# Inducing-point attention and routed experts in one pass: logits with tokens on partitions, PSUM as two pairs and four singles, eight chunks of x loaded a second time

## The chip, the cores and the metric

The kernel runs on one core of a Trainium2 chip. The metric is device time in microseconds of one execution; the median of several runs counts. Besides it there is one profiled execution with its trace.

## The reference

`x` is 4 batches of 10048 tokens with 128 channels in float32. 32 inducing vectors attend to all tokens of a batch (`h`), every token then attends to the 32 rows of `h`, and the result goes through a mixture of 16 experts in 4 groups, one expert a token:

```python
h = mab(I, x)            # softmax(scale * I @ x.T) @ x
y = mab(x, h)            # softmax(scale * x @ h.T) @ h
g_idx = argmax(y @ w_group); g_w = softmax(y @ w_group)[g_idx]
e_idx = argmax(y @ w_expert[g_idx]); e_w = softmax(y @ w_expert[g_idx])[e_idx]
out = g_w * e_w * (relu(y @ w1[g_idx, e_idx]) @ w2[g_idx, e_idx])
```

## The kernel before, in words

All arithmetic is float32. A batch is cut into J = 4 strands of 2512 tokens, and these into NK = 5 chunks of KW = 512 tokens; a chunk (b, k) holds 512 tokens of each strand, 1 MB. `xT` holds x with channels on partitions (this is loaded for every chunk, to `xk`, ten buffers), `xm` the same x with tokens on partitions.

Stage one (`att1`, `chunk`) of a chunk: scores of the inducing vectors (line 355), their running maximum (357, 362), the exponential on ScalarE with the sum of the weights in an accumulator (365), four transposes of the weights (373), and the weighted sums of x (391), which need x with tokens on partitions (`xn`, three buffers). Two chunks get `xn` from `xm` by DMA (`LOADED`); for the others `turn` transposes x on TensorE, 16 transposes in two halves (322), each half in two PSUM banks side by side, evicted by ScalarE or VectorE (294), whichever `sooner` names. After five chunks, `common` and `mean` make `hT`, and `routes` the small matrix `rbd` with the router's columns, 9 a strand (32 with padding). All tokens of a batch are expected to choose one expert: `routes` finds it from the mean, `expert` loads its weights, and makes, with the side of the ReLU that each hidden unit is on, a 32 x 128 matrix G (520, 532, 539, 543). Whether all of this holds for each token is checked on the way (counts on GpSimd, 602 to 611, `verdict`); a slow path stands behind for batches where it doesn't.

Stage two (`att2`) of a chunk: scores against `hT` (563), a transpose in blocks of 32 x 32 on VectorE (569), the maximum (573), its subtraction on GpSimd (575), the exponential (577), a second block transpose to `et` (580), the logits by one matmul with `rbd` as weights (585), and a third block transpose (593), after which tokens stand on partitions. `gates` turns logits of one or two chunks into one factor a token (626 to 646), and `outputs` multiplies the weights with it on GpSimd (655), transposes them (661), makes 4 matmuls of 512 columns with G (669) in four PSUM banks, evicts them (294) and writes 1 MB (678).

Nothing of this is in program order. `Plan` steps through generators, one for each job above; a job yields the engine that it wants next. `Pace` holds a modelled time for each engine, with a cost for each instruction; the plan takes the job that can start first, and among those that can start within a small window the one with the lowest key (batch and chunk number, with `LAG` = 9 chunks between a chunk's stage one and its stage two). What comes out is a fixed order for each engine (`in_order`). `Banks` hands out PSUM: four pairs of banks; a job takes a whole pair (`turn`, twice a chunk; `outputs`, two at once) or one bank of any pair, preferably one whose other half is taken:

```python
if n == 2:
    able = [(max(self.done(i, 0), self.done(i, 1)), i, 0) for i in range(4) if not (self.taken[i, 0] or self.taken[i, 1])]
```

Loads and stores all stand in SP's queue. At the start it issues batch 0's five chunks, `xm` of (0, 3) and (0, 4), and three chunks of batch 1; more loads of x are issued only once a first expert's weights have been asked for (`fetched`), then whenever a buffer comes free. SP also waits there for the expert's number (`value_load`, line 512).

Of the kernel before, what the change touches and what calls it, by code (L numbers as in the profile page):

```python
# [41 lines left out]
LOADED = {(0, 3), (0, 4)}  # L42
GROUPS = {b: [(0, 1), (2, 3), (4,)] for b in range(B)}
# [10 lines left out]
class Pace:  # L54
# [15 lines left out]
    def cost(self, i, n):  # L70
# [3 lines left out]
        if kind == "PE":  # L74
            n = math.prod([n for _, n in i.outs[0].ap[1:]])
            if "is_transpose=True" in str(i):
                return 0.11, 0.2
            c = max(0.025, n / 2400 + 0.0025) * (4 if i.ins[0].dtype == F32 else 1)
            rows, cols = i.ins[0].ap[0][1], i.outs[0].ap[0][1]
            return c / (4 if min(rows, cols) == 32 else 1), 0.2  # L80
        if kind == "POOL":
            return 0.1 + n / 500, 0.1
        if kind == "ACT":
            sides = [bool(self.span(x)) for x in i.ins[1:3]]
            return 0.1 + n / 1200 + 0.09 * sum(sides) + 0.2 * (len(outs) > 1), 0.15
        if kind == "DVE":
            return 0.07 + n / 960 + (0.08 if "Recip" in type(i).__name__ and n > 1 else 0.0), 0.13
# [113 lines left out]
class Banks:  # L201


    def __init__(self, pool, pace, pe):
        self.pairs = [pool.tile([P, 2 * KW], F32, name=f"ps{i}") for i in range(4)]
        self.taken = {(i, h): False for i in range(4) for h in range(2)}
        self.pace, self.pe, self.held = pace, pe, {}

    def done(self, i, h):
        return self.pace.idle(self.pairs[i].tensor.name, h * KW, h * KW + KW - 1)  # L210

    def take(self, n=1):
        asked = 0.0
        while True:
            now = max(self.pace.at.get(self.pe, 0.0), asked) + 0.05
            if n == 2:
                able = [(max(self.done(i, 0), self.done(i, 1)), i, 0) for i in range(4) if not (self.taken[i, 0] or self.taken[i, 1])]
            else:
                able = [(self.done(i, h), not self.taken[i, 1 - h], i, h) for (i, h), t in self.taken.items() if not t]
                soon = [x for x in able if x[0] <= now]  # L220
                able = [(t, i, h) for t, _, i, h in (sorted(soon, key=lambda x: (x[1], x[0])) or able)]
            if not able:
                yield
                continue
            t, i, h = able[0] if n == 1 and able[0][0] <= now else min(able)
            if t > now:
                asked = t
                yield t
                continue
            whole = self.pairs[i]  # L230
            tile_ = whole if n == 2 else whole[:, h * KW:(h + 1) * KW]
            for x in range(n):
                self.taken[i, h + x] = True
            self.held[id(tile_)] = tile_, [(i, h + x) for x in range(n)]
            return tile_

    def give(self, t):
        for x in self.held.pop(id(t))[1]:
            self.taken[x] = False


def fast(ctx, tc, xT, xm, wr, w1, w2, out, keep):
# [20 lines left out]
    xnring = Ring(cp, "xn", [P, TK, J, C], 3)  # L263
# [6 lines left out]
    lgring = Ring(cp, "lg", [P, 2, TQ, Q], 2)  # L270
    wring = Ring(cp, "w", [P, 2, TQ], 3)
# [4 lines left out]
    for r in rbd:  # L276
        nc.gpsimd.memset(r, 0.0)
# [5 lines left out]
    cnts = [tl([P, TQ, NL], f"cnt{i}") for i in range(2)]  # L283
    lows = [tl([P, len(GROUPS[b])], f"low{b}") for b in range(B)]

    xks, xns, hTs, hsums, rbds, Gs, es, lgs, ws = {}, {}, {}, {}, {}, {}, {}, {}, {}
    todo_x = list(CHUNKS)

    def sooner():

        return ACT if pace.at.get(ACT, 0.0) <= pace.at.get(DVE, 0.0) else DVE
# [4 lines left out]
    def load_xk(n=1):  # L296
        for _ in range(n):
            if todo_x and xring.tiles:
                b, k = todo_x.pop(0)
                t = xring.tiles.pop(0)  # L300
                nc.sync.dma_start(out=t, in_=xT[b, k])
                xks[b, k] = t

    def load_xn(b, k):
        t = xnring.tiles.pop(0)
        nc.sync.dma_start(out=t, in_=xm[b, k])
        xns[b, k] = t

    def turn(b, k):
# [6 lines left out]
        for half in range(2):  # L316
            ps = yield from banks.take(2)
            ts = range(half * TK // 2, (half + 1) * TK // 2)
            for i, t in enumerate(ts):
                tw = min(P, w - t * P)  # L320
                for j in range(J):
                    nc.tensor.transpose(ps[:tw, (i * J + j) * P:(i * J + j + 1) * P], xks[b, k][:, j, off + t * P:off + t * P + tw], ident)  # L322
            on = sooner()
            yield on
            full = sum((t + 1) * P <= w for t in ts)
            psv = ps.rearrange("p (t j c) -> p t j c", j=J, c=C)
            copy(on, xn[:, ts[0]:ts[0] + full], psv[:, :full])
            if full < len(ts):
                tw = w % P
                copy(on, xn[:tw, ts[-1]], psv[:tw, full])  # L330
            banks.give(ps)
            if half:
# [4 lines left out]
    def att1(b):  # L337
# [4 lines left out]
        if b < 2:  # L342
            small[i] = nbs, tl([P, 1], f"ssum{i}"), tl([P, C], f"hacc{i}"), [tl([P, 1], f"sm{i}{k}") for k in range(NK)], [tl([P, 1], f"cr{i}{k}") for k in range(NK)], tl([P, 1], f"mx{i}")
        nbs, ssum, hacc, sms, crs, mx = small[i]
        fcs = []

        def chunk(k):
# [10 lines left out]
            nb, sm, cr = nbs[k], sms[k], crs[k]  # L358
# [743 lines left out]
```

## Time and profile before

| | us |
|---|---|
| median of 3 runs | 262.26 (261.3 to 269.64) |
| the profiled execution | 261.98 |
| its span, first to last instruction | 260.1 |
| TensorE matmuls busy | 195.9 (75%) |
| VectorE busy | 175.0 (67%) |
| ScalarE busy | 98.7 (38%) |
| GpSimd busy | 60.8 (23%) |
| mean granted clock of TensorE | 0.881 |

Busy times are sums over the whole span; the kernel has stages of different kinds, so the sums are to be read stage by stage. The granted clock is 1.0 at 2.4 GHz and 0.5 at 1.2 GHz.

### The profile page before, as it was taken

The numbers are of one execution on the slowest core, as the hardware profiler recorded it, in microseconds if no ns is written. First come the engines' busy times: TensorE is split into PE (matmuls) and PEld (weight loads), VectorE is DVE, ScalarE is ACT, GpSimd is POOL, SyncE is SP. The second block draws the span as 40 slices with busy tenths as digits, with TensorE's granted clock in tenths as the row PEclk, the third lists the DMA queues.
The fourth block names the chain that finished last, engine by engine and source line by source line (L and its number), as shares of the span: only waits on it lengthen the run. The fifth ranks groups of instructions, "written<-read, shape, count | busy, mean of one in ns | idle before, by whom it ended". The sixth has DMA issues, their size and how long they took to land.

```text
span 260.1 us, 4501 instructions
## 1 busy us (share of the span) xinstructions
PE 195.9 (75%) x1705; PEld 107.3 (41%) x1705; DVE 175.0 (67%) x493; ACT 98.7 (38%) x173; POOL 60.8 (23%) x84
## 2 busy tenths in 40 slices
PE   0687889997989969979998583779979579475430
PEld 0253657653755745334755341234643352111100
DVE  0155647497767757888896959475886999946610
ACT  0444225435346343278620231336835106251420
POOL 0000000032113013432314134213360635344010
PEclk9999999999999988999999898555999959866755
DMA  6999300995003953599057000047343712816434
GB/s 216 427 425 422 160 0 4 319 420 233 3 0 111 372 190 140 178 394 377 8 210 277 0 0 0 1 165 323 161 149 163 267 59 101 355 53 282 202 129 152
DMA packets 12782, 48.42 MB, mean 186 GB/s; under 512 B 1104, under 2 KB 7376, under 8 KB 7888
## 3 DMA queue, kind: packets, MB, share of 16 engines
q1 hardware_dynamic: 12752, 48.05, 47.3%
q8 instruction: 15, 0.25, 0.4%
q14 instruction: 15, 0.12, 0.1%
HBM read 27.47 MB, written 20.58 MB: 185 GB/s over the span
## 4 chain that ended last, share of the span: by engine, by line
PE 48%; DVE 32%; issue 7%; ACT 6%; DMA 3%; SPq 0%; POOL 0%; ACTq 0%; DVEq 0%
PE ps L669 10%; PE ps L322 7%; PE ps L355 7%; PE ps L585 6%; PE ps L391 5%; PE ps L373 4%; PE ps L563 3%; DVE lg L593 3%; DVE mx L357 3%; ACT pe L365 3%; DVE et L580 2%; PE ps L520 2%; PE ps L539 2%; DMA xk<-xT 2%; DVE e L569 2%
## 5 line engine op out<-in xcount | busy, mean ns | idle before, releaser
L575 POOL TENSOR_TENSOR e<-e,mxe 128x512 f32<-128x512 f32 x20 | 20.9, 1047 | 106.8 <-DVE mxe L573 106.7
L669 PE MATMUL ps<-at,G 32*128 32x512 f32 x160 | 35.9, 832 | 9.9 <-DVE at L661 5.5
L294 ACT COPY osb<-ps 128x1024 f32<-128x1024 f32 x32 | 31.1, 1017 | 28.5 <-PE ps L669 18.9
L322 PE MATMUL ps<-cst,xk 128*128 128x128 f32 (+1 forms) x288 | 40.1, 285 | 0.0
L322 PEld LDWEIGHTS ps<-cst,xk 128*128 128x128 f32 (+1 forms) x288 | 33.1, 145 | 13.8 <-issue 8.9
L585 PE MATMUL ps<-et,rbd 128*128 128x512 f32 x40 | 26.4, 752 | 15.5 <-DVE et L580 15.2
L294 ACT COPY xn<-ps 128x1024 f32<-128x1024 f32 (+2 forms) x30 | 27.5, 925 | 25.3 <-PE ps L322 23.1
L655 POOL TENSOR_TENSOR e<-e,w 128x512 f32<-128x512 f32 x20 | 20.6, 1047 | 49.1 <-DVE w L646 49.1
L355 PE MATMUL ps<-xk,indT_sb 128*32 128x512 f32 (+1 forms) x160 | 22.7, 641 | 11.6 <-DMA xk<-xT 7.2
L365 ACT ACTIVATE pe<-ps,nb 128x512 f32<-128x512 f32 (+1 forms) x20 | 13.6, 679 | 34.6 <-DVE nb L362 9.1
L357 DVE TENSOR_REDUCE mx<-ps 128x1 f32<-128x512 f32 (+1 forms) x20 | 13.4, 671 | 17.1 <-PE ps L355 6.2
L391 PE MATMUL ps<-xn,pt 128*32 128x128 f32 (+1 forms) x640 | 21.7, 276 | 1.8 <-DVE xn L294 0.7
L563 PE MATMUL ps<-xk,hT 128*32 128x512 f32 x160 | 19.7, 599 | 2.9 <-ACT pe L365 2.0
L669 PEld LDWEIGHTS ps<-at,G 32*128 32x128 f32 x160 | 11.1, 240 | 25.9 <-issue 8.8
L391 PEld LDWEIGHTS ps<-xn,pt 128*32 128x32 f32 (+1 forms) x640 | 16.4, 109 | 9.3 <-issue 4.8
L569 DVE STREAM_TRANSPOSE e<-ps 128x512 f32<-128x512 f32 x20 | 14.0, 701 | 8.6 <-PE ps L520 3.4
L593 DVE STREAM_TRANSPOSE lg<-ps 128x512 f32<-128x512 f32 x20 | 14.1, 707 | 7.1 <-PE ps L585 1.9
L585 PEld LDWEIGHTS ps<-et,rbd 128*128 128x128 f32 x40 | 7.1, 221 | 25.8 <-DVE et L580 21.3
L661 DVE STREAM_TRANSPOSE at<-e 128x512 f32<-128x512 f32 x20 | 13.9, 698 | 5.1 <-PE ps L669 1.9
L577 ACT ACTIVATE e<-e 128x512 f32<-128x512 f32 x20 | 12.4, 629 | 12.4 <-POOL e L575 12.4
L373 PE MATMUL ps<-cst,pe 128*128 128x128 f32 x80 | 13.2, 295 | 2.7 <-ACT pe L365 1.1
L605 POOL TENSOR_SCALAR hit<-lg 128x128 f32<-128x128 f32 x16 | 8.5, 532 | 23.9 <-DVE lg L593 22.4
(109 smaller groups left out, 241.4 us busy)
## 6 DMA issues: line engine op xcount, KB each, us to landing
xk<-xT SPq DMA_DIRECT2D x20, 1024.0 KB, 8.5
out<-osb SPq DMA_DIRECT2D x16, 1024.0 KB, 3.9
out<-osb SPq DMA_DIRECT2D x4, 928.0 KB, 4.9
xn<-xm SPq DMA_DIRECT2D x2, 1024.0 KB, 15.6
w1s<-w SPq DMA_DIRECT2D x4, 512.0 KB, 3.7
w2s<-w SPq DMA_DIRECT2D x4, 512.0 KB, 6.0
cst<-consts SPq DMA_DIRECT2D x1, 178.5 KB, 2.4
indT_sb<-indT SPq DMA_DIRECT2D x1, 16.0 KB, 1.8
```

Source lines behind the costliest of these rows:

```text
L294: (nc.scalar.copy if engine == ACT else nc.vector.tensor_copy)(out=out, in_=in_)
L322: nc.tensor.transpose(ps[:tw, (i * J + j) * P:(i * J + j + 1) * P], xks[b, k][:, j, off + t * P:off + t * P + tw], ident)
L355: nc.tensor.matmul(ps[32 * j:32 * j + 32, :w], lhsT=indT_sb, rhs=xks[b, k][:, j, off:], start=True, stop=True)
L357: nc.vector.reduce_max(out=mx, in_=ps[:, :w], axis=AX.X)
L365: nc.scalar.activation(out=pe[:, :w], in_=ps[:, :w], func=AF.Exp, bias=nb, scale=SCALE, accum_out=sm)
L373: nc.tensor.transpose(ps[:tw, t * P:(t + 1) * P], pe[:, t * P:t * P + tw], ident)
L391: nc.tensor.matmul(hq[32 * j:32 * j + 32, 0:C], lhsT=pt[:tw, t, 32 * j:32 * j + 32], rhs=xn[:tw, t, j, :], start=(t == 0), stop=(t == nt - 1))
L563: nc.tensor.matmul(ps[32 * j:32 * j + 32, :], lhsT=hTs[b][:, 0:M], rhs=xks[b, k][:, j, :], start=True, stop=True)
L575: nc.gpsimd.tensor_tensor(out=e, in0=e, in1=mx[:, :, None].broadcast_to([P, TQ, M]), op=ALU.subtract)
L585: nc.tensor.matmul(ps, lhsT=rbds[b].rearrange("p j l -> p (j l)"), rhs=et, start=True, stop=True)
L593: nc.vector.transpose(out=slot.rearrange("p t l -> p (t l)"), in_=ps)
L669: nc.tensor.matmul((p0, p1)[j // 2][:, j % 2 * KW:(j % 2 + 1) * KW], lhsT=Gs[b][32 * j:32 * j + 32, :], rhs=at[32 * j:32 * j + 32, :], sta ...
```

## The change

- **Logits.** `et` becomes the weights of four matmuls with `rbd` (36 columns) moving; the result has tokens on partitions at once, 144 columns a chunk, and stays in one PSUM bank for a group of three chunks, then two. The third block transpose goes. The gates are then in another order than the weights that they multiply; four matmuls with an identity of 32 columns bring them back, and a copy takes them out of PSUM.
- **PSUM.** Two pairs and four single banks, each kind for its own takers.
- **x.** Chunks 1 and 3 of every batch come from `xm` too: 8 chunks, in two buffers of their own; `turn` has two buffers. Loads are issued in the order of use whenever a buffer is free, not after the first expert.
- **Sum of weights.** x with tokens on partitions has a 129th column of ones, so the weighted sums carry the sum of the weights; the accumulator and the running sums of VectorE go.
- **Expert.** The product for the second stage is made once, not for each strand; 32 matmuls by column groups take the place of eight.
- **Checks** are made once a group, in a job of their own. **Copies** go to ScalarE unless it is over 1 us behind VectorE. The planner's costs of instructions are other numbers.

```diff
-LOADED = {(0, 3), (0, 4)}
-GROUPS = {b: [(0, 1), (2, 3), (4,)] for b in range(B)}
+LOADED = {(b, k) for b in range(B) for k in (1, 3)}
+GROUPS = [(0, 1, 2), (3, 4)]
+GT = T * max(map(len, GROUPS))
+SPARE = 1.0
+PAIRS = 2
...
-            return c / (4 if min(rows, cols) == 32 else 1), 0.2
+            return max(0.06, c) / (4 if min(rows, cols) == 32 else 1) * 1.1, 0.2
         if kind == "POOL":
-            return 0.1 + n / 500, 0.1
+            return 0.36 + n / 740, 0.15
...
     def __init__(self, pool, pace, pe):
-        self.pairs = [pool.tile([P, 2 * KW], F32, name=f"ps{i}") for i in range(4)]
-        self.taken = {(i, h): False for i in range(4) for h in range(2)}
-        self.pace, self.pe, self.held = pace, pe, {}
+        self.free = {2: [pool.tile([P, 2 * KW], F32, name=f"pp{i}") for i in range(PAIRS)],
+                     1: [pool.tile([P, KW], F32, name=f"ps{i}") for i in range(8 - 2 * PAIRS)]}
...
+            t = min(free, key=self.done)
+            if self.done(t) > now:
+                asked = self.done(t)
+                yield asked
                 continue
+            free.remove(t)
+            return t
...
-    xnring = Ring(cp, "xn", [P, TK, J, C], 3)
+    xnring, xmring = Ring(cp, "xn", [P, TK, J, C + 1], 2), Ring(cp, "xm", [P, TK, J, C + 1], 2)
+    for t in xnring.tiles:
+        nc.gpsimd.memset(t[:, :, :, C:C + 1], 1.0)
...
-    mtring = Ring(cp, "mt", [P, FB, J, M], 1)
-    rbd = [tl([P, J, Q], f"rbd{i}") for i in range(2)]
+    mtring = Ring(cp, "mt", [P, FB, M], 1)
+    rbd = [tl([P, J, NL + 1], f"rbd{i}") for i in range(2)]
...
+    todo = [(what, *c) for c in CHUNKS for what in ("x", "n") if what == "x" or c in LOADED]
...
-        return ACT if pace.at.get(ACT, 0.0) <= pace.at.get(DVE, 0.0) else DVE
+        return ACT if pace.at.get(ACT, 0.0) <= pace.at.get(DVE, 0.0) + SPARE else DVE
...
+    def load():
+        for what, b, k in list(todo):
+            ring, src, have = (xring, xT, xks) if what == "x" else (xmring, xm, xns)
+            if not ring.tiles:
+                continue
+            todo.remove((what, b, k))
+            t = ring.tiles.pop(0)
+            nc.sync.dma_start(out=t, in_=src[b, k])
+            have[b, k] = t
...
-            nc.scalar.activation(out=pe[:, :w], in_=ps[:, :w], func=AF.Exp, bias=nb, scale=SCALE, accum_out=sm)
+            nc.scalar.activation(out=pe[:, :w], in_=ps[:, :w], func=AF.Exp, bias=nb, scale=SCALE)
...
-                    nc.tensor.matmul(hq[32 * j:32 * j + 32, 0:C], lhsT=pt[:tw, t, 32 * j:32 * j + 32], rhs=xn[:tw, t, j, :], start=(t == 0), stop=(t == nt - 1))
+                    nc.tensor.matmul(hq[32 * j:32 * j + 32, 0:C + 1], lhsT=pt[:tw, t, 32 * j:32 * j + 32], rhs=xn[:tw, t, j, :], start=(t == 0), stop=(t == nt - 1))
             ptring.give(pt)
-            xnring.give(xn)
+            (xmring if (b, k) in LOADED else xnring).give(xn)
+            load()
...
-                nc.vector.scalar_tensor_tensor(out=ssum, in0=ssum, scalar=cr, in1=sm, op0=ALU.mult, op1=ALU.add)
-                nc.vector.scalar_tensor_tensor(out=hacc, in0=hacc, scalar=cr, in1=hq[:, 0:C], op0=ALU.mult, op1=ALU.add)
+                nc.vector.scalar_tensor_tensor(out=hacc, in0=hacc, scalar=cr, in1=hq[:, 0:C + 1], op0=ALU.mult, op1=ALU.add)
...
-        fetched.add(b)
-        load_xk(XBUFS)
...
+        nc.vector.tensor_tensor(out=mt, in0=psv, in1=side[:, :, None].broadcast_to([P, FB, M]), op=ALU.mult)
...
-            nc.tensor.matmul(ps[:, 0:C], lhsT=mt[:, n].rearrange("p j m -> p (j m)"), rhs=w2s[:, n, :], start=(n == 0), stop=(n == FB - 1))
+            for j in range(J):
+                nc.tensor.matmul(ps[32 * j:32 * j + 32, 0:C], lhsT=mt[:, n, :], rhs=w2s[:, n, :], start=(n == 0), stop=(n == FB - 1))
...
-        if fetched:
-            load_xk()
+        load()
...
+        if (b, g) not in lgs:
+            lgs[b, g] = yield from banks.take()
+        lg, n = lgs[b, g], GROUPS[g].index(k)
+        for t in range(TK):
+            c = (n * TK + t) * J * (NL + 1)
+            nc.tensor.matmul(lg[:, c:c + J * (NL + 1)], lhsT=et[:, t * P:(t + 1) * P], rhs=rbds[b].rearrange("p j l -> p (j l)"), start=True, stop=True)
...
-        nc.tensor.matmul(ps, lhsT=rbds[b].rearrange("p j l -> p (j l)"), rhs=et, start=True, stop=True)
...
-        nc.vector.transpose(out=slot.rearrange("p t l -> p (t l)"), in_=ps)
...
+        nc.gpsimd.tensor_tensor(out=rq, in0=rs[:, :, None].broadcast_to([P, n * T, J]), in1=own_j[:, None, :, 0].broadcast_to([P, n * T, J]), op=ALU.mult)
...
+        nc.vector.tensor_tensor(out=wq, in0=pr[:, :, None].broadcast_to([P, n * T, J]), in1=rq, op=ALU.mult)
+        yield PE
         ps = yield from banks.take()
+        for j in range(J):
+            nc.tensor.matmul(ps[32 * j:32 * j + 32, 0:n * T], lhsT=same_m[:, 0:Q], rhs=wq.rearrange("p (t j) q -> p t j q", j=J)[:, :, j, :], start=True, stop=True)
+        w = yield from wring.take()
+        yield DVE
+        nc.vector.tensor_copy(out=w[:, 0:n * T], in_=ps[:, 0:n * T])
...
+        plan.add(checks(b, g, x, n), key(b, k) + LAG + 3.0, POOL, pace.at[DVE])
+    def checks(b, g, x, n):
+        cnt, parts = cnts[b % 2], x.rearrange("p (n t) l -> p n t l", n=n)
+        nc.gpsimd.tensor_scalar(x, x, 0.0, None, op0=ALU.is_ge)
...
-        p0 = yield from banks.take(2)
-        p1 = yield from banks.take(2)
+        n = min(PAIRS, 1) + 1
+        pss = []
+        for _ in range(J // n):
+            pss.append((yield from banks.take(n)))
```


## Rows read from the trace of the kernel before

**Rows 1.** The page: its first part's line of engines, and the slices' clock.

```profile
PE 195.9 (75%) x1705; PEld 107.3 (41%) x1705; DVE 175.0 (67%) x493; ACT 98.7 (38%) x173; POOL 60.8 (23%) x84
...
PEclk9999999999999988999999898555999959866755
```

**Rows 2.** Windows by stage: span, busy PE, PEld, DVE, ACT, POOL, clock, DMA, GB/s.

```profile
52.00:143.00 91.00, 81.48 (x822) 47.38 (x818) 71.06 (x207) 39.99 (x72) 23.69 (x30) 0.98 0.55 208
...
143.00:182.00 39.00, 28.06 (x121) 12.45 (x111) 27.58 (x66) 13.16 (x27) 10.79 (x13) 0.69 0.20 82
...
197.00:260.10 63.10, 35.44 (x157) 14.34 (x157) 40.37 (x116) 18.47 (x26) 19.32 (x24) 0.73 0.46 182
...
162.50:181.00 18.50, 15.00 (x47) 6.30 (x49) 10.40 (x20) 8.32 (x14) 4.71 (x5) 0.50 0.39 161
```

**Rows 3.** Timeline of PE (start, duration, line): 90 us, 133 to 178 us, 215 us.

```profile
90.01 2.05 PE L539 MATMUL ps<-w2s,mt 128*128 128x128 f32 x16
...
133.76 1.09 PE L322 MATMUL ps<-cst,xk 128*128 128x128 f32 x8
...
145.41 0.99 PE L355 MATMUL ps<-xk,indT_sb 128*32 128x464 f32 x8 [1.55 <-DVE big L534]
...
150.75 1.02 PE L585 MATMUL ps<-et,rbd 128*128 128x512 f32 x2
...
165.44 3.35 PE L669 MATMUL ps<-at,G 32*128 32x512 f32 x8
...
177.11 1.11 PE L322 MATMUL ps<-cst,xk 128*128 128x128 f32 x4
...
215.09 1.20 PE L669 MATMUL ps<-at,G 32*128 32x512 f32 x4
```

**Rows 4.** Timeline of DVE at 137, 204 and 241 us.

```profile
137.16 1.29 DVE L661 STREAM_TRANSPOSE at<-e 128x512 f32<-128x512 f32 x2
...
204.71 0.70 DVE L661 STREAM_TRANSPOSE at<-e 128x512 f32<-128x512 f32 x1
...
241.46 0.28 DVE L633 TENSOR_TENSOR x<-lg,rs 128x128 f32<-128x128 f32 x1
```

**Rows 5.** Timeline of ACT at 165 us and at the end.

```profile
165.61 0.65 ACT L365 ACTIVATE pe<-ps,nb 128x464 f32<-128x464 f32 x1 [4.46 <-PE ps L407]
...
243.89 0.33 ACT L636 ACTIVATE x<-x 128x128 f32<-128x128 f32 x1
...
251.37 1.93 ACT L294 COPY osb<-ps 128x1024 f32<-128x1024 f32 x2 [7.15 <-issue]
```

**Rows 6.** Groups by line and shape: count, busy us, mean ns, idle before them.

```profile
L322 PE MATMUL ps<-cst,xk 128*128 128x128 f32 x276 | 38.8, 286 | 0.0
...
L585 PE MATMUL ps<-et,rbd 128*128 128x512 f32 x40 | 26.4, 752 | 15.5 <-DVE et L580 15.2 <-DVE mx L357 0.3
...
L593 DVE STREAM_TRANSPOSE lg<-ps 128x512 f32<-128x512 f32 x20 | 14.1, 707 | 7.1 <-PE ps L585 1.9 <-PE ps L373 1.9 <-PE ps L355 0.9
...
L391 PE MATMUL ps<-xn,pt 128*32 128x128 f32 x608 | 20.8, 276 | 1.8 <-DVE xn L294 0.7 <-issue 0.5 <-DVE w L646 0.4
...
L539 PE MATMUL ps<-w2s,mt 128*128 128x128 f32 x64 | 11.3, 348 | 1.3 <-DVE e L569 1.1 <-DVE mt L532 0.2
...
L520 PE MATMUL ps<-hT,w1s 128*128 128x32 f32 x64 | 7.9, 277 | 2.5 <-DVE hacc L400 1.3 <-DMA w1s<-w 1.2
...
L532 DVE TENSOR_TENSOR mt<-ps,side 128x512 f32<-128x512 f32 x8 | 5.2, 686 | 0.1
...
L633 DVE TENSOR_TENSOR x<-lg,rs 128x256 f32<-128x256 f32 x8 | 3.5, 440 | 0.0
...
L449 DVE COPY hT<-ps 128x129 f32<-128x129 f32 x4 | 1.1, 288 | 0.5 <-PE ps L446 0.4
```

**Rows 7.** Timeline of PE's weight loads at 183 us.

```profile
183.20 0.86 PEld L322 LDWEIGHTS ps<-cst,xk 128*128 128x128 f32 x8 [0.20 <-issue]
```

**Rows 8.** The page's third part: the queue that moves tensors.

```profile
q1 hardware_dynamic: 12752, 48.05, 47.3%
```

More of the change, by code (lines that the diff above doesn't have):

```diff
@@ L204, in __init__, with done @@
     def __init__(self, pool, pace, pe):
-        self.pairs = [pool.tile([P, 2 * KW], F32, name=f"ps{i}") for i in range(4)]
-        self.taken = {(i, h): False for i in range(4) for h in range(2)}
-        self.pace, self.pe, self.held = pace, pe, {}
-    def done(self, i, h):
-        return self.pace.idle(self.pairs[i].tensor.name, h * KW, h * KW + KW - 1)
+        self.free = {2: [pool.tile([P, 2 * KW], F32, name=f"pp{i}") for i in range(PAIRS)],
+                     1: [pool.tile([P, KW], F32, name=f"ps{i}") for i in range(8 - 2 * PAIRS)]}
+        self.pace, self.pe = pace, pe
+    def done(self, t):
+        return self.pace.idle(t.tensor.name, 0, 2 * KW)
     def take(self, n=1):
-        asked = 0.0
+        asked, free = 0.0, self.free[n]
         while True:
             now = max(self.pace.at.get(self.pe, 0.0), asked) + 0.05
[L216 to L222, printed above, removed]
+            if not free:
                 yield
                 continue
[L225 to L228, printed above, removed]
+            t = min(free, key=self.done)
+            if self.done(t) > now:
+                asked = self.done(t)
+                yield asked
                 continue
[L230 to L235, printed above, removed]
+            free.remove(t)
+            return t
     def give(self, t):
-        for x in self.held.pop(id(t))[1]:
-            self.taken[x] = False
+        self.free[t.shape[1] // KW].append(t)
 def fast(ctx, tc, xT, xm, wr, w1, w2, out, keep):
@@ L315, in turn @@
         off, w = fresh(k)
[L316 to L320, printed above, removed]
+        n = min(PAIRS, 1) + 1
+        for t0 in range(0, TK, n):
+            ps = yield from banks.take(n)
+            tws = [min(P, w - t * P) for t in range(t0, t0 + n)]
+            for i, tw in enumerate(tws):
                 for j in range(J):
-                    nc.tensor.transpose(ps[:tw, (i * J + j) * P:(i * J + j + 1) * P], xks[b, k][:, j, off + t * P:off + t * P + tw], ident)
+                    at = off + (t0 + i) * P
+                    nc.tensor.transpose(ps[:tw, (i * J + j) * P:(i * J + j + 1) * P], xks[b, k][:, j, at:at + tw], ident)
             on = sooner()
             yield on
-            full = sum((t + 1) * P <= w for t in ts)
             psv = ps.rearrange("p (t j c) -> p t j c", j=J, c=C)
[L327 to L330, printed above, removed]
+            whole = sum(tw == P for tw in tws)
+            if whole:
+                copy(on, xn[:, t0:t0 + whole, :, 0:C], psv[:, :whole])
+            if whole < n:
+                copy(on, xn[:tws[-1], t0 + whole, :, 0:C], psv[:tws[-1], whole])
             banks.give(ps)
-            if half:
+            if t0 + n == TK:
                 xns[b, k] = xn
@@ L583, in att2 @@
         yield PE, pace.loaded(rbds[b])
-        ps = yield from banks.take()
-        nc.tensor.matmul(ps, lhsT=rbds[b].rearrange("p j l -> p (j l)"), rhs=et, start=True, stop=True)
-        etring.give(et)
-        yield DVE
-        g = next(i for i, v in enumerate(GROUPS[b]) if k in v)
-        if (b, g) not in lgs:
-            lgs[b, g] = (yield from lgring.take()), []
-        lg, done = lgs[b, g]
-        slot = lg[:, GROUPS[b][g].index(k)]
-        nc.vector.transpose(out=slot.rearrange("p t l -> p (t l)"), in_=ps)
@@ L626, in gates @@
+        rs, x, ex, s, pr, rq, wq = (t[:, :n * T] for t in gate_tiles[tag])
+        v = lg[:, 0:n * T * (NL + 1)].rearrange("p (t l) -> p t l", l=NL + 1)
         nc.vector.tensor_scalar_add(rs, v[:, :, NL], EPS)
         nc.vector.reciprocal(out=rs, in_=rs)
+        nc.vector.tensor_tensor(out=x, in0=v[:, :, 0:NL], in1=rs[:, :, None].broadcast_to([P, n * T, NL]), op=ALU.mult)
         nc.vector.tensor_reduce(out=lows[b][:, g:g + 1], in_=v[:, :, NL], axis=AX.X, op=ALU.min)
-        if g == len(GROUPS[b]) - 1:
+        banks.give(lg)
@@ L681, in verdict @@
     def verdict():
[L683 removed]
+        while len(proven) < B:
             yield
```

137 lines of the change are left out of this document (52 added, 85 removed).

## The prediction

> **What bounds the kernel now.** I read the page's shares first, then the windows by stage, then TensorE's and VectorE's timelines around the stage that looked worst, then the groups by line and shape for prices. The profiled execution took 261.98 us, its span 260.1 us with 1.9 us around it, and the median of the runs is 262.26 us, 0.3 us above it; sums are made against 261.98.
>
> TensorE is the busiest engine at 195.9 us, VectorE next with 175.0 us, ScalarE 98.7, GpSimd 60.8 [rows 1]. The average hides three stages [rows 2]. From 52 to 143 us TensorE is busy 81.48 of 91 us, 90%, at a granted clock of 0.98 (2.4 GHz nearly throughout): TensorE bounds this stage. From 143 to 182 us it is busy only 28.06 of 39 us at a clock of 0.69, and inside it, from 162.5 to 181 us, the clock is 0.50 (the 1.2 GHz level). From 197 us to the end it is 35.44 of 63.1 us: this is the last batch's chain, VectorE, ScalarE and waits in turn.
>
> The middle stage is the interesting one. Between the transposes at 133.76 us and the output matmuls at 165.44 us TensorE starts nothing that asks for two PSUM banks side by side, and the next transposes come at 177.11 us [rows 3]. The weights for output matmuls were ready long before: VectorE transposed them (two chunks) from 137.16 us on [rows 4]. By the code nothing is asked for between that transpose and the matmuls but the batch's matrix G, whose product ran at 90.01 us [rows 3], and two pairs of banks. I read this as single banks scattered over the four pairs: scores written at 145.41 us [rows 3] have their bank read by the exponential only at 165.61 us [rows 5]. The same shows later: transposed at 204.71 us [rows 4], output matmuls at 215.09 us [rows 3].
>
> **The change part by part.**
>
> (A float32 matmul leaves two records in the trace, a transpose one.)
>
> Turned chunks. 18 chunks are transposed now (276 + 12 transposes, 16 a chunk); 12 will be. One chunk costs 16 x 38.8/276 = 2.25 us of TensorE [rows 6], so six save 13.5 us, all in batches 1 to 3, hence mostly where TensorE is 90% busy: I count 12. With them go 12 evictions, which lay beside other work: 0. In exchange SP's queue issues six more loads of 1.06 MB. The queue's 48.05 MB take 47.3% of the span's engine time [rows 8], which is 390 GB/s while it is busy, 2.7 us a load. With more than half of the time free, and each load issued as soon as a buffer of the pair is given back, well ahead of its use, I cost them at nothing. If that cover goes, because SP stands in its wait for the expert's number with loads behind it, or loads stand ahead of the expert's weights, one load late is 2.7 us, once for each of three batches at most: 0 to +8 us, taken 0. At the start, batch 0's seven loads are the same bytes in another order, with a chunk to be transposed last: 0 to +2.7, taken 0.
>
> Logits. Each chunk's one matmul over 512 columns (26.4/20 = 1.32 us, of which the cold ones are the long ones) becomes four with 128-column weights and 36 moving columns. The nearest row is the expert's first stage, 128-column weights with 32 columns: 7.9/32 = 0.25 us, so 0.99 us a chunk; the second stage, 11.3/32 = 0.35 us, gives 1.41 [rows 6]. So -6.6 to +1.8 us for 20 chunks; the first row is nearer, but the old ones took 1.02 us where the clock was full (150.75 us [rows 3]), so I take -1. VectorE loses the 20 transposes of logits, 14.1 us [rows 6].
>
> Gates. Three groups a batch become two, with one more product written four times as wide, a swap by TensorE and a copy. The swap is four matmuls with 32-column weights and at most 48 columns; by the attention sums, 20.8/304 = 0.068 us each [rows 6], 8 x 0.27 = 2.2 us: +2. The copy lies below 0.29 us (128x129) [rows 6], 2.3 us for all. VectorE saves four rounds of nine small instructions, which at the 0.29 us of the copy row as the upper end is 0 to 10 us, and pays up to 2.3 for the copies and 8 x 0.44 [rows 6] at most for the wider product: -10 to +6, taken 0, and off the path in the middle. GpSimd's counting is regrouped, not cheaper; it was 23% busy, so it is free unless it stands in GpSimd's queue ahead of the last outputs: +1 at most.
> Between two tilings of the array, the weight load that follows 32-column weights at 183.20 us comes after 0.20 us idle, put down to issue [rows 7]. The Trainium skill's TensorEngine Tiling (Array Packing), Tiling Modes, says that changing the mode drains TensorE, which speaks against a swap by column tiles in the middle of full-array work; by it, with that 0.20 us twice for each of eight swaps, the sum would be 3.2 us higher, at 241. The trace agrees that there is such a gap.
>
> Weights' sum in x. The reader of ScalarE's accumulator goes (20 instructions, beside other work: 0), VectorE loses the running sums (one element a partition, 20 times: off the path, 0), and the attention sums stream 129 columns for 128: 1/128 of 20.8, +0.2. Expert: eight matmuls, 2.8 us a batch with cold ones in it, become 32 in column groups, 32 x 0.068 = 2.2: -0.6 to +0.2, taken 0; the product before them shrinks from 8 x 0.69 to 4 x 0.44 us [rows 6], 3.8 us less of VectorE.
>
> Copies. ScalarE is preferred by 1 us, so VectorE sheds copies. An exponential queued behind two more copies of 0.96 us waits 1.9 us [rows 5]; where that hurts is the tail, and the trace already has it there: x was ready at 241.74 us [rows 4] and its exponential ran at 243.89 us, behind copies [rows 5]. Bounds -5 to +4 for the whole kernel, taken 0.
>
> Truer costs in the planner change the order everywhere; no row prices that. -5 to +5, taken 0.
>
> PSUM as two fixed pairs and four singles. A single bank can no longer block a pair. In the stage 143 to 182 us TensorE's 28.06 us hold 15.0 us at half clock [rows 2], which are 7.5 at full clock, so 20.6 us of work; at 90% it fills 22.8 us: at best 16 saved. But VectorE's 27.58 us there, less four logit transposes (2.8), one expert product (0.9) and a few copies, are still 22 to 24; at the 78% that it reaches in 52 to 143 us (71.06 of 91) it needs 30, 9 saved. At worst 0: the wait moves to the singles. I take -10. VectorE's relief (175 to about 150 us in all) also fills some of TensorE's 9.5 idle us in 52 to 143: 0 to -6, taken -2.
>
> Tail, from 197 us. Saved: five logit transposes of 0.7 us of which half are on the path (-2), the expert's product (-0.9), and the batch-2 outputs that wait from 204.71 to 215.09 us and later push copies in front of the last exponentials (0 to -4, taken -2). Added: the last group is two chunks, not one, so a second chunk's evictions follow the last gates (1.93 us [rows 5]; with its 2.7 us of DMA behind them 4.6; taken +3), and the swap with its copy, +0.8. Sum -1.
>
> Together: -12 - 1 + 2 + 0.2 on TensorE, -10 - 2 for PSUM and VectorE's relief, -1 in the tail, -23.8 us: 261.98 - 23.8 = 238 us.
>
> **The rivals.**
>
> *Only the engine work goes* (chance 0.20): the stage at 143 us stalls again, for another reason, VectorE being its bound. For: VectorE is at 71% there while TensorE starves [rows 2], and its own chain would be what is late next. Then -10 and -2 both fall to 0: 250 us.
>
> *The clock takes it back* (0.16). In 143 to 182 us and after 197 us, where TensorE waits most, it spent much of the time at 1.2 GHz [rows 2]; with less to do it may fall to that level in 52 to 143 us too. One stretch like 162.5 to 181 us costs 7.5 us; two or three more bring 238 to 253 or 260.5; I give 258. Against: in its first 14 slices of 40 the page's row of the clock stays at 9, although TensorE waits there too [rows 1].
>
> *Four singles are too few* (0.10), the slower side. Per chunk the bare holds are: scores 1.1 + 0.7 + 0.2 + 0.7, weights' transposes 1.3, sums 1.4, second scores 1.8, expert's share 1.1: about 8.3 bank-us. The logits' bank is held over three chunks, then two; at 145 us for 15 chunks (52 to 197 us), 9.7 us each, that is about 7 more per chunk. Four banks offer 39. It decides once the bare holds are stretched 3.9-fold by waits; at five-fold a chunk takes (8.3 x 5 + 7)/4 = 12.1 us, 2.4 more for 15 chunks, 36 us: 238 + 36 = 274 us. For: the bank written at 145.41 us was held 21 us [rows 3, 5], eight-fold. Against: it was held so because other work came first, not by need, and a planner that sees no free bank finishes old work first.
>
> **How the numbers follow.** 0.54 on 238 us; 0.20, 0.16 and 0.10 on the rivals. The range runs from 223 (13.5 for the turned chunks, the best 16 for PSUM, 6 in 52 to 143 us and 3.5 of the tail's best) to 260, which takes in the first two rivals and leaves out the slow one and a little below. A measurement of this kernel tells about 2% from no change, 257.0 to 267.5 us. Faster by more: 0.54 + 0.20 + a part of the clock's: 0.77; within: 0.12; slower: 0.11.
>
> **What would show it.** Right: 192 transposes, some 27 us; no gap of tens of us between the transposes of output weights and the output matmuls; VectorE near 150 us, TensorE near 180; no stage of 39 us at a clock of 0.69. Wrong: score matmuls waiting for exponentials or sums of older chunks (singles); the clock row lower in the middle; TensorE waiting on loaded x; the last gates followed by more than 15 us. A time under 223 would mean that the planner's truer costs did much, which I priced at nothing.

## The result, and the profile after

The changed kernel takes 218.16 us (median of 4 runs, 215.38 to 222.37) against 263.01 us for the kernel before on the same chip: a ratio of 0.824, 95% interval [0.812, 0.836]. Two of the four runs, 219.27 and 222.37 us, fell in a slower state of the chip, and this ratio and all later ones compare runs outside it, while medians are over all runs. That is 45 us less, where 24 were forecast; 218 lies below the range's low end of 223 us. The profiled execution took 217.05 us, its span 215.3 us.

The page of the kernel after, its line of engines and the slices' clock, beside [rows 1]:

```profile
PE 182.1 (85%) x1985; PEld 111.7 (52%) x1985; DVE 132.1 (61%) x391; ACT 103.8 (48%) x164; POOL 60.8 (28%) x80
...
PEclk9999999999999999999999999967556955555555
```

The windows of the kernel after (span, busy PE, PEld, DVE, ACT, POOL, clock, DMA, GB/s): the stages of [rows 2], then from the last batch's `hT` to the end:

```profile
52.00:143.00 91.00, 88.18 (x1128) 56.78 (x1120) 70.71 (x213) 55.36 (x91) 33.84 (x40) 0.99 0.72 268
143.00:182.00 39.00, 32.74 (x216) 17.53 (x208) 27.47 (x79) 12.40 (x18) 16.19 (x20) 0.63 0.37 144
...
139.78:215.30 75.52, 54.54 (x307) 28.82 (x307) 39.04 (x112) 26.56 (x35) 25.99 (x32) 0.58 0.44 172
```

And the same last stretch of the kernel before, whose last `hT` stands at 196.48 us:

```profile
196.48:260.10 63.62, 35.93 (x161) 14.63 (x159) 40.53 (x117) 18.99 (x27) 19.32 (x24) 0.73 0.46 180
```

Of the 44.8 us that the span lost, TensorE's busy time gave 13.8 (195.9 to 182.1) and its idle time 31.0 (64.2 to 33.2, span less busy). From 52 to 143 us TensorE is now 97% busy at full clock. The last batch's `hT` comes 57 us sooner (196.48 to 139.78 us), but what follows it takes 12 us longer, 75.5 for 63.6, at a clock of 0.58 for 0.73. So 57 us were won and 12 given back.

Groups of the kernel after that answer to [rows 6] (count, busy us, mean ns, idle before them):

```profile
L284 ACT COPY osb<-pp 128x1024 f32<-128x1024 f32 x40 | 38.6, 1015 | 30.2 <-PE pp L660 15.6 <-issue 12.9 <-ACT ex L600 0.9
...
L574 PE MATMUL ps<-rbd,et 128*128 128x36 f32 x160 | 26.0, 320 | 3.1 <-DVE et L564 3.0
L311 PE MATMUL pp<-cst,xk 128*128 128x128 f32 x176 | 24.7, 283 | 0.4 <-DMA xk<-xT 0.4
L574 PEld LDWEIGHTS ps<-rbd,et 128*128 128x128 f32 x160 | 24.2, 234 | 9.3 <-DVE et L564 3.6 <-issue 1.7 <-DVE row L399 0.8
...
L525 PE MATMUL ps<-w2s,mt 128*32 128x128 f32 x256 | 9.4, 310 | 1.2 <-DVE big L519 1.2
...
L614 PEld LDWEIGHTS ps<-wq,cst 128*32 128x32 f32 x64 | 1.6, 120 | 6.2 <-DVE wq L610 3.7 <-issue 2.2 <-DVE e L553 0.3
L614 PE MATMUL ps<-wq,cst 128*32 128x48 f32 x32 | 1.3, 247 | 0.4 <-DVE wq L610 0.4
L614 PE MATMUL ps<-wq,cst 128*32 128x32 f32 x32 | 1.1, 215 | 0.9 <-DVE wq L610 0.9
```

The prices of TensorE's work were right: 192 transposes (176 here, 16 with 80 columns) take 27.1 us, logits 26.0 for 26.4, the swaps 2.4 where 2.2 were taken, the expert's second stage 9.4 for 11.3. What the sum did not foresee: all 40 output evictions are ScalarE's now (first row), and the wait for `et`, 15.2 us in [rows 6] and in no term of the sum, is 3.0 (second row).

### The profile page after: what moved, and what is told of

It reads as the page before. It is cut to its first block, busy times and chain, and to the rows that moved or that the text cites. A ratio compares the mean times of both kernels' runs of the same rounds, so it can differ in the third digit from the quotient of the medians.

```text
span 215.3 us, 4965 instructions
## 1 busy us (share of the span) xinstructions
PE 182.1 (85%) x1985; PEld 111.7 (52%) x1985; DVE 132.1 (61%) x391; ACT 103.8 (48%) x164; POOL 60.8 (28%) x80
## 5 line engine op out<-in xcount | busy, mean ns | idle before, releaser
L284 ACT COPY osb<-pp 128x1024 f32<-128x1024 f32 x40 | 38.6, 1015 | 30.2 <-PE pp L660 15.6
L660 PE MATMUL pp<-at,G 32*128 32x512 f32 x160 | 35.8, 838 | 4.8 <-DVE at L650 2.4
L284 ACT COPY xn<-pp 128x1024 f32<-128x1024 f32 (+2 forms) x28 | 24.5, 890 | 17.3 <-PE pp L311 17.3
L644 POOL TENSOR_TENSOR e<-e,w 128x512 f32<-128x512 f32 x20 | 20.4, 1048 | 39.8 <-DVE w L617 39.8
L574 PEld LDWEIGHTS ps<-rbd,et 128*128 128x128 f32 x160 | 24.2, 234 | 9.3 <-DVE et L564 3.6
L574 PE MATMUL ps<-rbd,et 128*128 128x36 f32 x160 | 26.0, 320 | 3.1 <-DVE et L564 3.0
L311 PE MATMUL pp<-cst,xk 128*128 128x128 f32 (+1 forms) x192 | 26.3, 282 | 0.4 <-DMA xk<-xT 0.4
L311 PEld LDWEIGHTS pp<-cst,xk 128*128 128x128 f32 (+1 forms) x192 | 21.6, 143 | 9.0 <-issue 6.1
L347 DVE TENSOR_REDUCE mx<-ps 128x1 f32<-128x512 f32 (+1 forms) x20 | 13.5, 673 | 15.1 <-PE ps L345 15.1
L564 DVE STREAM_TRANSPOSE et<-e 128x512 f32<-128x512 f32 x20 | 14.0, 701 | 3.0 <-ACT e L561 3.0
L650 DVE STREAM_TRANSPOSE at<-e 128x512 f32<-128x512 f32 x20 | 13.5, 695 | 1.6 <-POOL e L644 1.5
L557 DVE TENSOR_REDUCE mxe<-e 128x16 f32<-128x512 f32 x20 | 13.4, 670 | 0.2
L381 PE MATMUL ps<-xn,pt 128*32 128x129 f32 (+1 forms) x384 | 13.1, 275 | 0.0
```

The costliest lines, as they stand in the source:

```text
L284: (nc.scalar.copy if engine == ACT else nc.vector.tensor_copy)(out=out, in_=in_)
L381: nc.tensor.matmul(hq[32 * j:32 * j + 32, 0:C + 1], lhsT=pt[:tw, t, 32 * j:32 * j + 32], rhs=xn[:tw, t, j, :], start=(t == 0), stop=(t == ...
L564: nc.vector.transpose(out=et, in_=e.rearrange("p t m -> p (t m)"))
L574: nc.tensor.matmul(lg[:, c:c + J * (NL + 1)], lhsT=et[:, t * P:(t + 1) * P], rhs=rbds[b].rearrange("p j l -> p (j l)"), start=True, stop=True)
L644: nc.gpsimd.tensor_tensor(out=e, in0=e, in1=w[:, i * T:(i + 1) * T, None].broadcast_to([P, T, M]), op=ALU.mult)
L650: nc.vector.transpose(out=at, in_=e.rearrange("p t m -> p (t m)"))
```

## The experiments

All kernels stand against the kernel before, run on the same chip (medians 262.75 to 264.36 us); ratios have 95% intervals. Five parts of the change can be set one by one: *banks* (two fixed pairs, four singles), *preference* (copies to ScalarE unless it is 1 us behind), *loads* (eight chunks and the order of loads), *costs* (the planner's numbers), and *arithmetic* (logits, swap, column of ones, expert). The parts are not quite clean: every kernel with the new arithmetic also has the new order of loads, two buffers for turned chunks and two for loaded ones, even where only two chunks are loaded; and the kernels with loads but the old arithmetic have nine buffers for x in place of ten. What the order of loads and the buffers are worth by themselves was not measured, but for the tenth buffer in the kernel after. The theory at first was that the banks did more than their 10 us; one rival, from the prediction's last sentence, that the truer costs did; another, that the loaded chunks gave far more than their 12 us.

**Banks alone, costs alone** (the kernel before with the diff's `class Banks`, or its `cost`, and nothing else):

```diff
+PAIRS = 2
-        self.pairs = [pool.tile([P, 2 * KW], F32, name=f"ps{i}") for i in range(4)]
+        self.free = {2: [pool.tile([P, 2 * KW], F32, name=f"pp{i}") for i in range(PAIRS)],
+                     1: [pool.tile([P, KW], F32, name=f"ps{i}") for i in range(8 - 2 * PAIRS)]}
...
```

> Before, with PSUM as two pairs and four singles and nothing else. Theory 1 (the fixed pairs end the wait of output matmuls for pairs; the 10 us of the forecast were too few): 240 to 252 us, and no gap of 25 us between the transposes of output weights and the output matmuls. Theory 2 (the planner's truer costs are what was left out): 257 us or more. Theory 3 (the loaded chunks give far more than their 12 us, because turning takes pairs, evictions and waits too): 255 us or more, since all 18 chunks are still turned.

> Before, with the planner's new costs of instructions alone. Theory 2: 242 us or less. Theories 1 and 3: 255 to 268 us, the order changes but pairs are still blocked by single banks.

Banks alone: 247.08 us, 0.941 [0.935, 0.947], 16 us less. Costs alone: 268.62 us, 1.019 [1.013, 1.025], 5 us more. The rival of the costs falls.

The trace of banks alone: the prediction's stage, for [rows 2], and what is left to win, as a window and timelines of PE, DVE and ACT.

```profile
143.00:182.00 39.00, 32.50 (x255) 17.87 (x243) 32.62 (x91) 14.59 (x27) 11.80 (x15) 0.87 0.31 118
...
100.00:119.00 19.00, 13.64 (x151) 7.71 (x149) 17.28 (x59) 5.29 (x13) 6.91 (x8) 0.95 0.63 218
...
101.89 1.97 PE L312 MATMUL pp<-cst,xk 128*128 128x128 f32 x16
...
122.78 2.09 PE L659 MATMUL pp<-at,G 32*128 32x512 f32 x8
...
102.08 0.66 DVE L651 STREAM_TRANSPOSE at<-e 128x512 f32<-128x512 f32 x1
...
104.08 1.23 DVE L284 COPY xn<-pp 128x1024 f32<-128x1024 f32 x1
...
118.84 1.19 DVE L284 COPY xn<-pp 128x1024 f32<-128x1024 f32 x1
...
118.39 0.69 ACT L355 ACTIVATE pe<-ps,nb 128x512 f32<-128x512 f32 x1 [6.54 <-DVE nb L352]
```

From 143 to 182 us TensorE is busy 32.50 us at a clock of 0.87, for 28.06 at 0.69 before. Earlier in the same trace, the 16 transposes at 101.89 us fill both pairs. VectorE copies one at 104.08 and the other only at 118.84 us, behind other work in its order that keeps it 91% busy (17.28 of 19 us); ScalarE is busy 5.29 us and waits. The output matmuls take both pairs at once, so output weights transposed at 102.08 us are used only at 122.78. No small taker blocks a pair here; the queue of the engine that is to empty it does.

**Undone from the kernel after: loads, banks, costs, preference.**

```diff
-LOADED = {(b, k) for b in range(B) for k in (1, 3)}
+LOADED = {(0, 3), (0, 4)}
```

> After, with only chunks (0, 3) and (0, 4) loaded a second time, so six more chunks are turned. By the forecast's step (six chunks at 2.25 us of TensorE): 217 + 12 to 14 = 229 to 231 us. Theory 3: 237 us or more. If loads were hidden and turning too: under 222 us.

239.34 us, 0.908 [0.902, 0.915]: 21 us more than after, more than the turned chunks' work, as the theory of the loaded chunks had it; a later run takes that back.

> After, with the shared pool of four pairs of before, of which single banks can block any. Theory 1: 230 us or more, with gaps of 10 us and more before output matmuls while their weights are ready. Theories 2 and 3: 217 to 223 us. If four singles were too few in the changed kernel, this would be faster than 215.

(The class `Banks` of before.) 256.98 us, 0.979 [0.971, 0.988]: 39 us more.

> After, with the planner's old costs of instructions. By themselves the new costs gave nothing. If they matter once PSUM and loads are as in the changed kernel: 224 us or more. If the order that comes out is as good with either: 214 to 221 us.

219.73 us (216.1 to 223.3, no ratio): no difference from after that can be told.

```diff
-SPARE = 1.0
+SPARE = 0.0
```

> After, with copies given to ScalarE only when it is free before VectorE, as before. If a pair's time is spent waiting for an eviction that VectorE's order puts behind other work (seen with fixed pairs alone: a pair written at 103.9 us, evicted by VectorE at 118.84 us, with output matmuls ready from 102.8 us and run at 122.78 us), this gives 225 us or more, with waits of over 10 us between transposes of output weights and output matmuls. If copies don't matter, as the forecast took it: 214 to 221 us.

233.77 us, 0.891 [0.884, 0.898]: 16 us more. VectorE takes 11 copies out of pairs again (none after) and is busy 145.1 us for 132.1. The longest stretch between a transpose of output weights and their matmuls was some 7 us, though (99.22 to 105.81 us), so the waits of 10 us and more that the expectation named are not how the 16 us are made up.

**Added step by step.** The kernel before with banks and loads; then with preference and costs too (all but the arithmetic). Both have nine buffers for x.

> Before, with fixed pairs and singles and with the 8 loaded chunks in the new order of loads, nothing else; nine buffers of x. If the two add up as measured singly (16.5 us for the pairs alone, 22 us for loading when it is taken out of the changed kernel): 223 to 229 us. If each needs the rest of the change (truer costs, ScalarE preferred, less work on VectorE): 234 us or more.

> Before, with all of the change that is not arithmetic: fixed pairs and singles, the new costs, ScalarE preferred, 8 chunks loaded and the new order of loads, but logits transposed by VectorE, sums by the accumulator and the expert's product as before. Nine buffers of x in place of ten, for the room that the padded logits take. If the forecast's prices of the arithmetic hold (a few us): 217 to 224 us. If VectorE's relief of some 30 us carries a good part of the gain: 230 us or more.

240.25 us, 0.912 [0.904, 0.919], and 229.66 us, 0.876 [0.869, 0.884].

**Loads alone, preference alone**, each on the kernel before:

```diff
-        return ACT if pace.at.get(ACT, 0.0) <= pace.at.get(DVE, 0.0) else DVE
+        return ACT if pace.at.get(ACT, 0.0) <= pace.at.get(DVE, 0.0) + SPARE else DVE
```

> The kernel before with eight chunks of x loaded untransposed instead of two, and nothing else of the change but the order of those loads. If the 13.5 us that TensorE no longer spends on turning six chunks are on the path by themselves, 249 to 251 us. If the pairs that stand blocked set the pace of the kernel before, TensorE only gets to the same waits sooner: 255 to 263 us.

> The kernel before with the planner's preference for ScalarE as taker of copies, and nothing else. If the preference works by giving fixed pairs back quickly, it needs the fixed pairs, and alone brings at most 5 us: 257 to 268 us. If it works by relieving VectorE, which is the same with any banks, 252 us or less.

Loads alone: 268.87 us, 1.030 [1.018, 1.042], 5 us more. Preference alone: 248.37 us, 0.947 [0.935, 0.960], 15 us less, with the shared pairs of before. So it does not need the fixed pairs, and as the expectation has it, that speaks for the relief of VectorE. Loads alone came out above both forecasts; it also has nine buffers for x and the smaller buffers for turned chunks, whose share of the 5 us is not known. The page of loads alone, and its mean clock (0.881 before):

```profile
PE 195.1 (73%) x1609; PEld 102.4 (38%) x1609; DVE 173.8 (65%) x490; ACT 89.2 (33%) x165; POOL 60.6 (23%) x84
...
core 0: 266.7 us, clock 0.829
```

TensorE has 96 transposes less and is busy 195.1 us for 195.9: nearly all of the 13.5 us came back as work at the lower clock, and its idle time rose from 64.2 to 71.6 us.

**Parts of the arithmetic, and no pairs at all.** The kernel after with the accumulator's sums and the four-fold expert product of before (nine buffers for x); and with single banks only:

```diff
-PAIRS = 2
+PAIRS = 0
```

> The kernel after with the column of ones and the expert product put back as they were, so that of the arithmetic only the logits with tokens on partitions and the gates' swap are left; nine buffers for x. It stands between 229.7 us (everything but the arithmetic) and 218 us (all). If the logits carry the gain of the arithmetic, 217 to 221 us; if the sum of weights and the expert product carry it, 226 us or more.

> The kernel after with no pair at all: all eight banks single, every eviction of one bank, so there are more and smaller evictions. If what counts is only that no small taker blocks a pair, 215 to 222 us, for there is no pair to block. If the pairs are worth keeping because one wide eviction costs its engine less than two, 225 us or more.

Logits kept: 222.16 us, 0.849 [0.841, 0.857], between the two forecasts. Beside the kernel after with nine buffers too, which follows below (222.11 us), nothing is left for the column of ones and the expert product that can be told. No pairs: 227.81 us, 0.869 [0.858, 0.880], 10 us more than after, in place of 39 with the shared pairs. So some 29 of those 39 us go where no pair can be blocked, and the pairs themselves are worth the rest. The remaining 10 are not the engines' own price of smaller copies: ScalarE is busy 105.2 us for 103.8, VectorE 135.2 for 132.1. What they are was not found.

**Are banks and preference one thing or two? Is the arithmetic worth anything without them?** The second kernel has the arithmetic, the order of loads and the buffers of after and, from before, `Banks`, `cost`, `SPARE = 0.0` and two loaded chunks.

> The kernel before with the two fixed pairs and four singles and the preference for ScalarE, nothing else. Alone the banks brought 16 us and the preference 15. If both only shorten the time that a bank is held, they overlap: 242 to 250 us. If the banks end the blocking of pairs and the preference relieves VectorE, two separate things, they add: 230 to 236 us.

> The kernel before with the logits, the gates' swap, the column of ones and the expert product as after, and with the banks, the planner and the two loaded chunks as before (x rings and load order as after). Added last to all the rest, these brought 11 us. If VectorE's work stands between TensorE's starts whatever the banks do, they bring about as much alone: 248 to 254 us. If the pairs set the pace of the kernel before, VectorE's saving is swallowed: 259 to 268 us.

Banks with preference: 224.57 us, 0.852 [0.844, 0.860]: 39 us less, more than the 16 and 15 added up, and below both forecasts. Arithmetic alone: 246.41 us, 0.933 [0.924, 0.943], 17 us less, more than either forecast. The page of banks with preference, its clock and two stages:

```profile
PE 186.1 (84%) x1705; PEld 103.9 (47%) x1705; DVE 155.5 (70%) x468; ACT 115.3 (52%) x198; POOL 61.4 (28%) x84
...
core 0: 222.3 us, clock 0.886
...
52.00:143.00 91.00, 88.77 (x931) 53.65 (x927) 75.38 (x234) 60.96 (x107) 30.55 (x38) 0.98 0.60 214
143.00:182.00 39.00, 31.27 (x192) 14.92 (x188) 32.43 (x95) 15.84 (x26) 16.38 (x21) 0.87 0.38 146
```

It has the 1705 matmul records of [rows 1], not one piece of TensorE's work less. Idle time fell from 64.2 to 36.2 us, busy time by 9.8, and from 52 to 143 us TensorE is 98% busy. VectorE is busy 155.5 us, for 178.2 with banks alone, and makes 4 copies out of pairs for 19. How much of what the preference brings is pairs given back sooner, and how much is VectorE's other work coming sooner, no run separates: the pair held until 118.84 us above speaks for the first, the gain with shared pairs for the second.

**Nine buffers, and the last gates first.**

```diff
-            plan.add(gates(b, g), key(b, k) + LAG + 0.3, DVE, pace.at[PE])
+            plan.add(gates(b, g), key(b, k) + LAG + 0.3 - (4 if b == B - 1 else 0), DVE, pace.at[PE])
```

> The kernel after with nine buffers for x instead of ten, the number that the kernels with the old arithmetic and eight loaded chunks have. If the tenth buffer does nothing, 216 to 220 us, and what stands between those kernels and the one after is arithmetic; if TensorE waits for x with nine, 222 us or more, and that share of the gap is the buffer's.

> The kernel after with the gates of the last batch four places earlier in the planner's order. Behind the last gates the kernel after has some 18 us, most of it output matmuls at half clock. If the gates' chain is what is late at the end, 211 to 215 us. If TensorE's remaining work sets the end, whatever goes first, 216 to 220 us.

Nine buffers: 222.11 us, 0.836 [0.823, 0.850], whose interval overlaps that of after: not told apart. Gates first: 224.34 us, 0.852 [0.845, 0.859], some 7 us slower than after by the ratios; both forecasts miss. The edit did not bring the last gates forward: their swap, at 196.29 us in the kernel after, now comes later, with 18.8 us of the span of 222.7 behind it.

```profile
203.91 0.34 PE L614 MATMUL ps<-wq,cst 128*32 128x32 f32 x8 [3.27 <-DVE wq L610]
```

So what earlier gates would bring stays open. A small edit of the order is worth 7 us by itself, so smaller steps between the kernels here are not to be explained.

**The last corners.** Banks and preference with the arithmetic alone (the kernel after with `LOADED` and `cost` of before), and with the loads alone:

> The kernel after with two loaded chunks and the planner's costs as before, so the kernel before with banks, preference and arithmetic. Banks and preference alone stand at 224.6 us. If the arithmetic takes its 17 us off there too, 205 to 214 us, faster than the kernel after, and loads and costs are what holds that one back. If in that company TensorE's own work is what is left, which the arithmetic doesn't lessen, 219 to 228 us. With the truer costs instead this kernel took 239 us; if the turned chunks, not the costs, made that, 235 us or more.

> The kernel before with banks, preference and the eight loaded chunks, costs and arithmetic as before, nine buffers for x. Without the loads it stands at 224.6 us, with loads and the truer costs at 229.7 us. If the turned chunks' 13.5 us are on TensorE's path once it is 97% busy, 211 to 216 us. If loads bring nothing without the arithmetic, 222 to 232 us.

216.67 us, 0.828 [0.820, 0.837], and 217.93 us, 0.830 [0.824, 0.835]: both as fast as the whole change, and each between its two forecasts. The first one, and beside it the kernel that differs from it in the planner's costs alone (239.34 us, above):

```profile
PE 186.6 (87%) x2081; PEld 120.2 (56%) x2081; DVE 132.2 (61%) x393; ACT 114.0 (53%) x173; POOL 60.9 (28%) x80
...
core 0: 215.2 us, clock 0.883
...
52.00:143.00 91.00, 88.55 (x1058) 57.80 (x1051) 67.94 (x202) 59.35 (x94) 33.38 (x39) 0.98 0.63 231
```

```profile
PE 196.3 (83%) x2081; PEld 126.3 (53%) x2081; DVE 136.5 (57%) x395; ACT 111.2 (47%) x171; POOL 60.8 (26%) x80
...
core 0: 237.6 us, clock 0.838
...
52.00:143.00 91.00, 83.93 (x992) 57.16 (x984) 61.32 (x177) 48.80 (x79) 27.09 (x31) 0.92 0.55 196
```

The same 2081 matmul records: with the truer costs TensorE is busy 9.7 us longer at the lower clock and idles 41.3 us for 28.6.

## Why the prediction was wrong

Medians in us, with what else is as before:

| | alone | + loads | + arithmetic | + both |
|---|---|---|---|---|
| the kernel before | 263 | 268.9 | 246.4 | |
| banks | 247.1 | 240.3 | | |
| costs | 268.6 | | | |
| preference | 248.4 | | | |
| banks and preference | 224.6 | 217.9 | 216.7 | 219.7 |
| banks, preference, costs | | 229.7 | 239.3 | 218.2 |

Banks and preference gained in every company in which they were run: banks 16 us alone, 24 on top of the preference and 39 in the kernel after; preference 15 alone, 23 on top of the banks and 16 in the kernel after. No other part did so in all of its company. Every part also changes the planner's order, and the costs, which change nothing else, moved the time by up to 23 us; so the sign of these two is shown, and their sizes, like the steps of 5 to 8 us below, hold for these kernels' orders.

**PSUM, taken as -10.** The mechanism was right and the term mis-sized: 16 us alone. The bound of -16 was worked out for the stage from 143 to 182 us; in company the term is larger (24 and 39 us). That single banks block pairs is borne out by the kernel after with shared pairs, 39 us slower, beside the one with no pairs to block, 10 us slower.

**"Copies", taken as 0 with bounds of -5 to +4: this step failed.** The preference is worth 15 us alone and 16 when it is taken out of the kernel after. The prediction priced only what more copies do to ScalarE's queue; what fewer do to VectorE's it had at most within the -2 of VectorE's relief. There a pair is held until its copy comes up, 15 us after the transposes at 101.89 us in the run shown above, while ScalarE was busy 5.29 of 19 us. The kernel before has 17 such copies of pairs on VectorE, 20.4 us of its 175.0, and the kernel after none:

```profile
L294 DVE COPY xn<-ps 128x1024 f32<-128x1024 f32 x9 | 10.9, 1216 | 2.1 <-PE ps L322 1.2 <-ACT osb L294 0.9
L294 DVE COPY osb<-ps 128x1024 f32<-128x1024 f32 x8 | 9.5, 1205 | 0.0
```

Together banks and preference bring 39 of the 45 us, where the prediction had -10 for the one and 0 for the other: 29 us more, while the whole sum was 21 us short. The Trainium skill's TensorEngine Tiling (Array Packing), PSUM Bottleneck, advises to use both ScalarE and VectorE for evicting PSUM. The runs set a condition to it for this kernel: where VectorE has other work, giving each copy to the engine that is free first cost 16 us more than preferring ScalarE (233.77 beside 218.16).

**VectorE's relief, taken as -2 (0 to -6).** Also mis-sized for the arithmetic: 17 us alone, with VectorE's busy time at 161.0 for 175.0 us. On top of banks and preference it is 8. Both figures hold the new order of loads and its buffers too, which no run takes apart from it. In the kernel after VectorE stands at 132.1 us, not near 150.

**Turned chunks, taken as -12: this step failed in its place, though not in its price.** The transposes take 13.5 us less, as priced (27.1 us for 40.6), but 5 us were lost in the kernel before, 7 won on top of banks and preference, and nothing where the arithmetic is there too (219.7 beside 216.7). The rival "the clock takes it back" was the true course of loads alone: twice (1 - clock) x span, an estimate of the time at 1.2 GHz from the runs' clocks, goes from 62 to 91 us. The undoing from after (21 us) misled: the two kernels with the same two loaded chunks but the costs of before and after stand at 216.7 and 239.3.

**Truer costs, taken as 0 with bounds of -5 to +5, and "a time under 223 would mean that the planner's truer costs did much".** That sentence was wrong, and so were the bounds: the costs lose 5 us in the kernel before, and on top of banks and preference 12 with the loads, 23 with the arithmetic, and nothing that can be told with both. Why they order the work worse in three of four companies stays open; the runs show only that TensorE then waits more.

**Tail, taken as -1.** What follows the last `hT` grew by 12 us, with 54.5 us of TensorE's work in it for 35.9. The prediction's sign "no stage of 39 us at a clock of 0.69" did not come: from 143 to 182 us the clock is 0.63, now within this last stretch. The end is as "more than 15 us behind the last gates" described it; the last swap and the last work, timelines of PE and ACT after:

```profile
196.29 0.34 PE L614 MATMUL ps<-wq,cst 128*32 128x32 f32 x8
196.60 3.00 PE L660 MATMUL pp<-at,G 32*128 32x512 f32 x8
...
203.50 2.58 PE L660 MATMUL pp<-at,G 32*128 32x512 f32 x8
...
205.67 1.93 ACT L284 COPY osb<-pp 128x1024 f32<-128x1024 f32 x2 [1.72 <-PE pp L660]
```

Nearly 19 us of the span lie behind the swap at 196.29 us, with the clock's slices at 0.5 throughout. Whether earlier gates would shorten it is not known. That the tail is why loads and arithmetic don't add is argued from the last `hT` (its matmul at 156.51 us with banks, preference and arithmetic, at 139.78 after, with the same span), not shown by a run that removes it.

**Right:** the prices of all of TensorE's work, 192 transposes in 27 us, and no gap of tens of us ahead of the output matmuls. TensorE near 180 us (182.1) was in part luck: banks and preference took 9.8 us off its busy time without a matmul less, and with them and the arithmetic, all 18 chunks turned, it stood at 186.6 already. Of four singles being too few there is no sign. The Trainium skill's TensorEngine Tiling (Array Packing), Tiling Modes, by which draining at mode changes was to cost 3.2 us, is not refuted: the swaps' weight loads have 2.2 us of idle put down to issue ahead of them. But those of the logits have 1.7 us of it too, so that the 2.2 are the price of the mode is not shown.

No kernel here beats the one after by more than the measurement can tell; banks, preference and arithmetic with two loaded chunks are as fast, and so are banks, preference and loads.

## What to carry to other kernels

The hold of a PSUM bank can include the queue of the engine that empties it, as the 15 us above do: price a rule for who copies by what it does to the engine that sheds the copies, not only to the one that takes them, and look for a pair whose copy waits while another engine idles. Parts of a change need not add up, in either direction (16 and 15 us made 39; 7 from the loads and 8 from the arithmetic did not make 15); so size the likeliest pair together, and measure parts in the company that they will have. Work taken from an engine that waits may buy nothing while the waits stand: 13.5 us of transposes bought none in the kernel before.

## What was not expected of the hardware

- TensorE's busy time is no measure of its work: the same 1705 matmul records take 195.9 us in the kernel before and 186.1 with banks and preference, and 96 transposes less took off 0.8 us, as the mean clock went from 0.881 to 0.829.
- Eighty matmuls of 36 columns (26.0 us) cost TensorE what twenty of 512 did (26.4), each at the clocks that its kernel had, with as much weight loading beside them as matmul: 24.2 us at 234 ns a record. What was saved is VectorE's third transpose.
- The same 128x1024 copy takes 1.01 us on ScalarE and 1.22 on VectorE (1217 ns, twelve copies in banks alone).
